# Four tiles in turn for the softmax statistics, and GpSimd and VectorE in ScalarE's place for the early normalisation

## The chip, the cores and the metric

The kernel runs on one core of a Trainium2 chip. The metric is the device time of one execution in microseconds (us), given as the median of several runs; lower is better. A profiled execution gives the trace, from which the rows further down are taken. The engines are named as the profile names them: PE is TensorE, ACT is ScalarE, DVE is VectorE, POOL is GpSimd, and SP is SyncE, which only issues transfers here. Each engine works through its own instructions strictly in order.

## The reference

Three stages follow one another: attention over a band of 64 keys, a gated feed-forward layer, and a second feed-forward layer with a leaky activation.

```python
# q, k, v: 4 batches, 8 heads, 576 positions, 64 wide
scores = (q @ k.T) / sqrt(64)                       # per batch and head
scores = where(0 <= pos_q - pos_k < 64, scores, -1e9)
attn = exp(scores - max(scores)); attn /= sum(attn) + 1e-9
x = (attn @ v)  -> 2304 tokens x 512
x = (silu(x @ w_gate) * (x @ w_val)) @ w_out        # 512 -> 1536 -> 512
h = x @ w2_in                                       # 512 -> 2048
out = maximum(0.01 * h, h) @ w2_out                 # 2048 -> 512
```

The weights arrive in 64-bit floats.

## The kernel before

**Attention in jobs.** The 2304 tokens are cut into five blocks of up to 512 columns. The attention of a block is done by eight jobs (one for a pair of heads and a part of the block). Jobs 0 to 7 make the first block and are the early ones: nothing else can begin before them. Their tokens are two halves of 256: jobs 0 to 3 make part 0, jobs 4 to 7 part 1. A job is a chain of steps over four tiles of 128 by 128:

- `natural` transposes q and k on PE and copies the result out of PSUM (on DVE for jobs 0, 1, 4, 5, on ACT for the others).
- `scores` (L210 to L229) multiplies on PE (L221), adds the mask and takes the row maxima on DVE (L226, called the reduction below), and on ACT takes the exponential with the row sums (L228). Maxima go to row 0 and sums to row 1 of a small tile `st`.
- `norm` (L231 to L243) adds 1e-9 to the sums (L235), takes the reciprocal (L236), both on DVE, and multiplies each of the four tiles by it: on ACT (L239), DVE (L241) or POOL (L243).
- `transpose` turns the tiles on PE (L249) and ACT copies them out (L253); `values` multiplies by v on PE (L266) and writes x (ACT L275, DVE L276).

**Buffers of a job.** The score tiles `e`, the transposed q and k and the transposed scores of an early job lie in one of four sets of rooms, in turn. The statistics tile `st` has one buffer for all jobs. In PSUM, jobs 0 to 3 have a bank each; all that jobs 4 to 7 put into PSUM, with the q and k transposes and the v products of every job, goes through one pair of buffers named `att`.

**The first feed-forward layer.** Its weights come in 36 tiles, three (gate, value, out) for each of the 12 slices f of the hidden width. A weight tile is fetched by SP into one of three raw buffers (L292), made into 32-bit floats by ACT (L302) and DVE (L304, L305), and split into a high and a low half by ACT (L312) and DVE (L313). A step (part, f) on PE is twelve matmuls for gate (pg), twelve for value (pv) and twelve for the output (acc), all on L560; between them ACT and DVE make the gated product (L604, L605, L612, L614), and POOL its low half (L615). In the first block the order of steps is (0,0), (0,1), (0,2), (0,3), (0,4), (1,0), (0,5), (1,1), (0,6), and so on to (1,11), so part 1 of x is first needed at the sixth step.

**What sets the order.** Each piece of work has a due time in slots (three slots to a step). A planner places each engine's instructions by these due times and its own reckoning of when each is ready. In `scores`, `norm`, `transpose` and `values` the work that is not PE's is moved ahead by 9.4 slots (`soon`), so that attention goes before weight tiles where both are ready.

**The later attention** (jobs 8 and up) shares one set of rooms for `e` in any case, and is normalised on ACT or, in some jobs, on POOL.

Of the kernel before, what the change touches and what calls it, by code (L numbers as in the profile page):

```python
# [8 lines left out]
F32 = mybir.dt.float32  # L9
# [4 lines left out]
P = 128  # L14
# [13 lines left out]
def banded_attention_moe_moe(  # L28
# [12 lines left out]
    nc = tc.nc  # L41
# [28 lines left out]
    ap = ctx.enter_context(tc.tile_pool(name="ap", bufs=1))  # L70
# [61 lines left out]
    def soon():  # L132
        prio(now[0] - 9.4)

    def load_nat(b, src, a, h0, h1, queue=nc.sync):
        for m in range(2):
            queue.dma_start(out=nat[:, a, m, h0:h1],
                              in_=src[b, h0:h1, m * P:(m + 1) * P, :].rearrange("h p d -> p h d"))

    def load_nv(b):  # L140

        for i in range(3):
            nc.sync.dma_start(out=nv[i], in_=v[b, :, 64 * i:64 * i + P, :].rearrange("h p d -> p h d"))

    def in_turn(mm):

        tc.keep_in_program_order(mm)

    class Job:
# [59 lines left out]

        def scores(self, i):  # L210
            if i == 0:
                self.st = ap.tile([P, 4, 6], F32, tag="st", name="st")
            st, e = self.st, self.e
            ps = (ps_acc if self.n < 4 else ps_att).tile([P, 4, P], F32, tag=self.bank, name="s")
            for a, t in enumerate(self.fills[i]):
                w0 = 64 * (t if self.half else max(t - 1, 0))
                if not self.early:
                    in_turn(nc.tensor.matmul(ps[:, a], lhsT=qbd[:, t, :], rhs=kT[:, w0:w0 + P], start=True, stop=True))  # L218
                    continue
                for r in (slice(0, 64), slice(64, 128)):  # L220
                    nc.tensor.matmul(ps[r, a], lhsT=self.kq[r, 256 + 64 * t:320 + 64 * t], rhs=self.kq[r, w0:w0 + P],  # L221
                                     start=True, stop=True)
            soon()
            for a, t in enumerate(self.fills[i]):
                mask = masks[:, 1 if (t == 0 and not self.half) else 0, :]
                nc.vector.tensor_tensor_reduce(out=e[:, t], in0=ps[:, a], in1=mask, scale=-0.125, scalar=3.0e38,  # L226
                                               op0=ALU.add, op1=ALU.min, accum_out=st[:, 0, t:t + 1])
                nc.scalar.activation(e[:, t], e[:, t], AF.Exp, bias=st[:, 0, t:t + 1], scale=-1.0,  # L228
                                     accum_out=st[:, 1, t:t + 1])  # L229

        def norm(self, i, engine):  # L231
            soon()
            ts, st, e = self.fills[i], self.st, self.e
            a, z = ts[0], ts[-1] + 1
            nc.vector.tensor_scalar(st[:, 2, a:z], st[:, 1, a:z], 1.0e-9, None, op0=ALU.add)  # L235
            nc.vector.reciprocal(st[:, 3, a:z], st[:, 2, a:z])  # L236
            for t in ts:
                if engine is nc.scalar:
                    nc.scalar.activation(e[:, t], e[:, t], AF.Copy, scale=st[:, 3, t:t + 1])  # L239
                elif engine is nc.vector:  # L240
                    nc.vector.tensor_scalar(e[:, t], e[:, t], st[:, 3, t:t + 1], None, op0=ALU.mult)  # L241
                else:
                    nc.gpsimd.tensor_scalar(e[:, t], e[:, t], st[:, 3, t:t + 1], 1.0, op0=ALU.mult, op1=ALU.mult)  # L243
# [245 lines left out]
    for blk, members in enumerate(BLOCKS):  # L489
        for n in range(2 * HP):  # L490
            i, hp = (n // HP, n % HP) if blk == 0 else (n % 2, n // 2)
# [6 lines left out]
    def at(slot, fn):  # L498
        plan.append((slot, len(plan), fn))
# [12 lines left out]
    for n, j in enumerate(jobs):  # L512
        nxt = jobs[n + 1] if n + 1 < len(jobs) else None
        if j.early:
            t = 2.4 * min(n, 4) + 3 * max(0, n - 4)
            E = lambda r, f, t=t: at(t + r - 17.3, f)
            E(0.0, j.natural)
            E(1.5, lambda j=j: j.scores(0))
            E(4.6, lambda j=j: j.norm(0, (nc.vector, nc.gpsimd, nc.scalar)[min(j.n, 2)]))
            E(6.3, lambda j=j: j.transpose(0))  # L520
            E(7.8, j.values)
            if n == 3:
                E(0.1, lambda: [load_nat(1, src, a, 0, H) for src, a in ((k, 0), (q, 1))])
                E(7.9, lambda: load_nv(1))
            if n == 7:
                E(7.9, nxt.load)
                E(7.9, lambda n=n: [jobs[n + a].load_v(True) for a in (1, 2)])
            continue
        i = n - min(jj.n for jj in jobs if jj.blk == j.blk)
        b0 = FIRST[j.blk - 1] + int(4.5 * i) + (29 if j.blk == 1 else -5)  # L530
        L = lambda r, f, b0=b0: at(b0 + r, f)
        L(0, j.quadrants)
        if nxt:
            L(0, nxt.load)

        s, m, t, w = (2, 4, 5.6, 8.7) if j.blk == 1 else (1.2, 3, 4.4, 7.2)
        for i in range(len(j.fills)):
            L(s + 0.4 * i, lambda j=j, i=i: j.scores(i))
            on = nc.scalar if j.blk > 1 or j.T < 5 else nc.gpsimd
            L(m + 0.2 * i, lambda j=j, on=on, i=i: j.norm(i, on))  # L540
            L(t + 0.2 * i, lambda j=j, i=i: j.transpose(i))
        if j.first:
            L(w, j.values)
            if nxt:
                L(w, lambda n=n: [jobs[n + a].load_v() for a in (1, 2)])
# [94 lines left out]
    for blk in range(1, NBLK):  # L640
        for f in range(NF1):
            slot = FIRST[blk] + 3 * f
            step1(slot, blk, slice(0, WIDTH[blk]), f, f == 0, f == NF1 - 1)
            i = NF1 * (blk - 1) + f
# [170 lines left out]
    for n, (i, fp) in enumerate(units):  # L815
# [19 lines left out]
        if n == 1:  # L835
            for j in (10, 11):
                space[j] = wp.tile([P, 3072], F32R, tag=f"w{j}", name=f"space{j}")
        t = {k: pool.tile([P, 448 if pool is tp else 512], F32, tag=tag, name=k)[:, 0:HALF]
             for k, pool, tag in (("t1", tp, "t"), ("u2", up, "u"), ("t5", tp, "g0"), ("u3", up, "u"), ("c", tp, "g1"))}
# [112 lines left out]
```

## Time and profile before

| | |
|---|---|
| median of 3 runs | 931.12 us (930.8 to 931.42) |
| profiled execution, its own time | 928.26 us |
| its span, first to last instruction | 926.3 us |
| PE busy in the span | 906.5 us (98%) |
| DVE, ACT, POOL busy | 662.3, 473.1, 350.5 us |
| mean granted clock of PE | 0.994 |

The span is the stretch that the trace covers, and all times in the rows are counted from its start. The profiled execution's own time lies 1.96 us over its span, and 2.86 us under the median.

### The profile page before, as it was taken

What the parts mean: (1) busy time and instruction counts of PE and PEld (TensorE: products, weight loads), DVE (VectorE), ACT (ScalarE), POOL (GpSimd) and SP (SyncE); (2) the same over time, 40 slices, a digit from 0 to 9 for tenths busy, and PEclk for the clock granted to TensorE, in tenths of its full rate; (3) what the DMA queues carried; (4) which work ended last, traced back from release to release, by engine and by line L of the source; (5) the groups of instructions that cost most, each with busy time, mean ns of one, the idle gap of its engine ahead of it and who ended that gap; (6) DMA issues with size and microseconds to landing.
All of it is one profiled execution on the core that took longest, in us unless ns stands there. A gap on an engine that the chain in (4) does not pass through costs nothing.

```text
span 926.3 us, 18141 instructions
## 1 busy us (share of the span) xinstructions
PE 906.5 (98%) x6147; PEld 858.6 (93%) x6147; DVE 662.3 (72%) x1529; ACT 473.1 (51%) x1181; POOL 350.5 (38%) x492
## 2 busy tenths in 40 slices
PE   7899899999999999999999999999999999999998
PEld 5788899999999999999999999999999999999997
DVE  5889854456666566656654464899998999978787
ACT  6976644545555555545543344635545445454342
POOL 1021322112122212222222123866668556675555
PEclk9899999999999999999999999999999999999999
DMA  9787433336566666656545694887559874588752
GB/s 245 209 221 232 130 56 59 90 85 187 185 195 169 206 193 176 195 163 179 168 162 190 250 319 134 265 252 243 160 178 294 263 249 128 165 268 265 246 159 80
DMA packets 198524, 176.32 MB, mean 190 GB/s; under 512 B 118048, under 2 KB 146976, under 8 KB 198432
## 3 DMA queue, kind: packets, MB, share of 16 engines
q1 hardware_dynamic: 196288, 174.64, 62.1%
q8 instruction: 49, 0.80, 0.4%
q10 hardware_dynamic: 2144, 0.52, 0.3%
q14 instruction: 43, 0.35, 0.1%
HBM read 135.27 MB, written 39.85 MB: 189 GB/s over the span
## 4 chain that ended last, share of the span: by engine, by line
PE 90%; DMA 4%; ACT 2%; DVE 2%; issue 1%; POOL 0%; ACTq 0%; SPq 0%; DVEq 0%; POOLq 0%
PE pg L560 15%; PE pv L560 15%; PE acc L560 15%; PE y L720 13%; PE px L677 8%; PE pw L677 5%; PE py L677 5%; PE yc L720 5%; DMA raw<-in_moe_w_val_dram 3%; PE s L218 3%; PE pv L266 2%; PE pt L249 2%; DMA raw<-in_moe_w_out_dram 1%; PE s L221 1%; DVE u L305 1%
## 5 line engine op out<-in xcount | busy, mean ns | idle before, releaser
L615 POOL TENSOR_TENSOR g<-th,g 128x448 fp32r<-128x448 f32 (+1 forms) x72 | 78.5, 1090 | 313.4 <-ACT g L614 284.6
L560 PE MATMUL pv<-x,w 128*128 128x448 f32 (+1 forms) x864 | 174.3, 345 | 4.9 <-DVE th L612 2.9
L560 PE MATMUL pg<-x,w 128*128 128x448 f32 (+1 forms) x864 | 172.4, 344 | 4.7 <-ACT x L275 3.0
L560 PE MATMUL acc<-g,w 128*128 128x448 f32 (+1 forms) x864 | 167.7, 340 | 1.6 <-POOL g L615 1.3
L560 PEld LDWEIGHTS pg<-x,w 128*128 128x128 f32 x864 | 144.1, 190 | 15.1 <-ACT x L275 3.4
L560 PEld LDWEIGHTS pv<-x,w 128*128 128x128 f32 x864 | 143.1, 190 | 15.7 <-DVE th L612 4.0
L560 PEld LDWEIGHTS acc<-g,w 128*128 128x128 f32 x864 | 144.5, 189 | 12.1 <-POOL g L615 2.5
L720 PE MATMUL y<-space,g 128*128 128x256 f32 x1035 | 145.6, 282 | 0.0
L720 PEld LDWEIGHTS y<-space,g 128*128 128x128 f32 x1035 | 137.9, 190 | 0.5 <-DVE space L714 0.3
L714 DVE TENSOR_TENSOR space<-y,space 128x512 f32<-128x512 f32 (+1 forms) x180 | 102.5, 593 | 11.5 <-PE y L720 10.7
L699 POOL TENSOR_TENSOR g<-t,g 128x384 fp32r<-128x384 f32 x71 | 77.9, 1099 | 56.5 <-ACT g L698 44.6
L677 PE MATMUL px<-space,space 128*128 128x384 f32 x432 | 89.1, 337 | 0.0
L605 DVE SCALAR_TENSOR_TENSOR th<-th,pg 128x448 f32<-128x448 f32 (+1 forms) x72 | 39.7, 551 | 62.1 <-ACT th L604 61.6
L677 PEld LDWEIGHTS px<-space,space 128*128 128x128 f32 x432 | 74.2, 188 | 1.0 <-DVE t L909 0.6
L614 ACT CAST g<-th 128x448 fp32r<-128x448 f32 (+1 forms) x72 | 37.0, 513 | 65.7 <-DVE th L612 65.7
L302 ACT ACTIVATE u<-raw 128x512 f32<-128x512 f32 x68 | 45.8, 676 | 47.8 <-DMA raw<-in_moe_w_out_dram 15.9
L699 POOL TENSOR_TENSOR g<-c,g 128x384 fp32r<-128x384 f32 x47 | 50.7, 1079 | 39.0 <-ACT g L698 26.9
L720 PE MATMUL yc<-space,g 128*128 128x256 f32 x414 | 63.7, 281 | 0.0
L677 PE MATMUL py<-space,space 128*128 128x384 f32 x288 | 63.5, 336 | 0.0
L677 PE MATMUL pw<-space,space 128*128 128x384 f32 x288 | 62.8, 336 | 0.0
L228 ACT ACTIVATE e<-e,st 128x128 f32<-128x128 f32 x120 | 46.9, 392 | 26.1 <-DVE st L226 26.1
L304 DVE TENSOR_SCALAR raw<-raw 128x512 int32<-128x512 int32 x68 | 29.4, 433 | 42.2 <-ACT u L302 34.1
(145 smaller groups left out, 1479.8 us busy)
## 6 DMA issues: line engine op xcount, KB each, us to landing
space<-o SPq DMA_DIRECT2D x147, 256.0 KB, 3.4
space<-a SPq DMA_DIRECT2D x140, 256.0 KB, 3.7
raw<-in_moe_w_out_dram SPq DMA_DIRECT2D x28, 512.0 KB, 4.9
a<-hl SPq DMA_DIRECT2D x24, 512.0 KB, 3.0
o<-hl SPq DMA_DIRECT2D x24, 512.0 KB, 3.1
raw<-in_moe_w_in_dram SPq DMA_DIRECT2D x16, 512.0 KB, 4.7
raw<-in_moe_w_gate_dram SPq DMA_DIRECT2D x12, 512.0 KB, 4.3
raw<-in_moe_w_val_dram SPq DMA_DIRECT2D x12, 512.0 KB, 4.7
```

The source lines that it names most:

```text
L218: in_turn(nc.tensor.matmul(ps[:, a], lhsT=qbd[:, t, :], rhs=kT[:, w0:w0 + P], start=True, stop=True))
L228: nc.scalar.activation(e[:, t], e[:, t], AF.Exp, bias=st[:, 0, t:t + 1], scale=-1.0, accum_out=st[:, 1, t:t + 1])
L302: nc.scalar.activation(u, f32(high), AF.Prelu, scale=EXP_SCALE, alpha=NEGATIVE)
L304: nc.vector.tensor_single_scalar(part, low, 29, op=ALU.logical_shift_right)
L560: nc.tensor.matmul(ps, lhsT=w(a, c), rhs=x(b, c), start=(start and n == 0), stop=(stop and n == 3 * len(cs) - 1), skip_group_check=True)
L605: nc.vector.scalar_tensor_tensor(out=th, in0=th, scalar=1.0, in1=pg, op0=ALU.add, op1=ALU.mult)
L614: nc.scalar.copy(g[0][:, :n], th)
L615: nc.gpsimd.tensor_tensor(g[1][:, :n], th, f32(g[0][:, :n]), op=ALU.subtract)
L677: nc.tensor.matmul(ps, lhsT=A2[n, k][:, a, c * P:c * P + P], rhs=X2[i, c, k][:, b], start=start and m == 0, stop=m == 5, skip_group_check= ...
L699: (lo or nc.gpsimd).tensor_tensor(g[:, 1], src, f32(g[:, 0]), op=ALU.subtract)
L714: nc.vector.tensor_tensor(f32(dst), ps, f32(dst), op=ALU.add)
L720: nc.tensor.matmul(ps, lhsT=g[:, a, r * P:r * P + P], rhs=O2[n, k][:, b], start=start and m == 0, stop=m == 2, skip_group_check=True)
```

## The change

The statistics tile gets four names in turn, by the job's number modulo 4, so that four jobs can each have one. The normalisation of a job takes a list of four engines, one for each tile, instead of one engine. Job 0 keeps DVE for its four tiles. Jobs 1 to 3 take POOL, DVE, POOL, DVE (job 1 had POOL for all four, jobs 2 and 3 had ACT). Jobs 4 to 7 take POOL for all four (they had ACT). The later jobs keep the engines that they had.

```diff
             if i == 0:
-                self.st = ap.tile([P, 4, 6], F32, tag="st", name="st")
+                self.st = ap.tile([P, 4, 6], F32, tag=f"st{self.n % 4}", name="st")
...
-        def norm(self, i, engine):
+        def norm(self, i, engines):
             soon()
...
-            for t in ts:
+            for t, engine in zip(ts, engines):
...
-            E(4.6, lambda j=j: j.norm(0, (nc.vector, nc.gpsimd, nc.scalar)[min(j.n, 2)]))
+            engines = [nc.vector] * 4 if n == 0 else [nc.gpsimd, nc.vector] * 2 if n < 4 else [nc.gpsimd] * 4
+            E(4.6, lambda j=j, engines=engines: j.norm(0, engines))
...
-            L(m + 0.2 * i, lambda j=j, on=on, i=i: j.norm(i, on))
+            L(m + 0.2 * i, lambda j=j, on=on, i=i: j.norm(i, [on] * 4))
```

## Rows read from the trace of the kernel before

**Rows 1.** The page: busy times, and busy tenths in 40 equal slices.

```profile
PE 906.5 (98%) x6147; PEld 858.6 (93%) x6147; DVE 662.3 (72%) x1529; ACT 473.1 (51%) x1181; POOL 350.5 (38%) x492
...
DVE  5889854456666566656654464899998999978787
ACT  6976644545555555545543344635545445454342
```

**Rows 2.** Stages: length, busy time of each engine, granted clock, DMA share, GB/s.

```profile
15.00:40.00 25.00, 18.28 (x151) 14.62 (x149) 20.79 (x71) 24.14 (x75) 0.99 (x2) 0.80 0.85 219
40.00:65.00 25.00, 23.12 (x210) 20.97 (x206) 22.50 (x62) 22.06 (x63) 5.49 (x8) 1.00 0.78 220
65.00:110.00 45.00, 40.73 (x317) 38.48 (x318) 39.98 (x89) 29.45 (x66) 10.54 (x14) 1.00 0.70 210
110.00:926.00 816.00, 812.24 (x5368) 774.49 (x5367) 572.51 (x1279) 389.62 (x960) 330.12 (x448) 1.00 0.61 187
```

**Rows 3.** PE's waits from 15 to 66.4 us: total, times, longest.

```profile
PE pg L560 <- ACT x L275: 3.0, 2, 2.6
PE pv L560 <- ACT w L312: 2.1, 1, 2.1
PE pv L560 <- DVE th L612: 1.2, 2, 0.6
```

**Rows 4.** PE's timeline: start, length, instruction (scores of jobs 3, 5, 7; steps).

```profile
12.70 0.43 PE L221 MATMUL s<-rooms 64*64 64x128 f32 x2
...
30.02 1.09 PE L221 MATMUL s<-nat 64*64 64x128 f32 x16
...
48.48 1.09 PE L221 MATMUL s<-rooms 64*64 64x128 f32 x16
...
61.46 1.70 PE L560 MATMUL pv<-x,w 128*128 128x256 f32 x12 [0.60 <-DVE th L612]
...
66.36 1.36 PE L560 MATMUL pg<-x,w 128*128 128x256 f32 x10
```

**Rows 5.** DVE's timeline: first reductions of jobs 3, 5, 7; one weight split.

```profile
21.28 0.29 DVE L226 CUSTOM_DVE_ANT_0 rooms<-s,masks 128x128 f32<-128x128 f32 x1 [0.49 <-ACT rooms L239]
...
34.33 0.29 DVE L226 CUSTOM_DVE_ANT_0 nat<-s,masks 128x128 f32<-128x128 f32 x1
...
50.72 0.29 DVE L226 CUSTOM_DVE_ANT_0 rooms<-s,masks 128x128 f32<-128x128 f32 x1
...
57.90 0.65 DVE L313 TENSOR_TENSOR w<-u,w 128x512 fp32r<-128x512 f32 x1
```

**Rows 6.** ACT's timeline: job 2's normalisation and what follows it.

```profile
19.97 1.28 ACT L239 ACTIVATE rooms<-rooms,st 128x128 f32<-128x128 f32 x4
21.15 0.60 ACT L312 CAST w<-u 128x512 fp32r<-128x512 f32 x1
```

**Rows 7.** One stage for L239 alone: length, ACT busy, clock, DMA share, GB/s.

```profile
15.00:60.00 45.00, 7.79 (x24) 0.89 0.81 218
```

**Rows 8.** Single lines: shortest, median, longest ns; first and last start.

```profile
L241 DVE TENSOR_SCALAR e<-e,st x4: 280/282/286, 9.7 to 10.3; 128x128 f32<-128x128 f32 x4
...
L243 POOL TENSOR_SCALAR nat<-nat,st x4: 369/377/802, 14.1 to 15.6; 128x128 f32<-128x128 f32 x4
...
L313 DVE TENSOR_TENSOR w<-u,w x36: 648/686/1240, 14.6 to 110.3; 128x512 fp32r<-128x512 f32 x36
```

**Rows 9.** POOL's timeline: job 1's normalisation, and a later low half.

```profile
14.13 1.86 POOL L243 TENSOR_SCALAR nat<-nat,st 128x128 f32<-128x128 f32 x4 [10.98 <-ACT pT L253]
...
107.20 1.02 POOL L615 TENSOR_TENSOR g<-th,g 128x256 fp32r<-128x256 f32 x1 [1.27 <-ACT g L614]
```

**Rows 10.** DVE's timeline beside these two stretches of POOL.

```profile
14.56 0.83 DVE L313 TENSOR_TENSOR w<-u,w 128x512 fp32r<-128x512 f32 x1 [0.62 <-ACT w L312]
...
106.00 0.43 DVE L304 TENSOR_SCALAR raw<-raw 128x512 int32<-128x512 int32 x1 [1.36 <-DMA raw<-in_moe_w_val_dram]
...
107.55 0.96 DVE L304 TENSOR_SCALAR raw<-raw 128x512 int32<-128x512 int32 x1
```

## The prediction

> **What bounds the kernel now.** I read the page first. PE is busy for 98% of the span, so over the whole run it is the bound, and the other engines matter only where they make PE wait. ACT's and DVE's slices are fullest at the left edge [rows 1], so I asked next for stages. From 110 us to the end PE is busy for 812.24 of 816 us at full clock [rows 2]: nothing that the change does there can shorten more than 3.8 us. What can be gained lies before 110. From 15 to 65 us PE is idle for 50 - 18.28 - 23.12 = 8.6 us, and from 65 to 110 for 4.3 us. In the first of these stages the granted clock is 0.80 on average: part of the stretch runs at the lower of the two levels, 1.2 GHz. At full clock its 18.28 busy us could be as little as 18.28 x 0.80 = 14.6, so the clock holds at most another 3.7 us. The ceiling of any gain before 65 us is thus 8.6 + 3.7 = 12.3 us.
>
> The waits of PE in that stage come next. The longest are for x, the output of the early attention (ACT L275, 3.0 us), and for a weight half that ACT had not made yet (2.1 us) [rows 3]. Both come from ACT, which is busy for 24.14 + 22.06 = 46.2 of the 50 us, and in 15 to 40 for 24.14 of 25 [rows 2]: ACT's queue sets the pace there. DVE is close behind, with 43.3 of 50.
>
> The timelines of PE and DVE show the second cause, which no list of waits names well. The score matmuls of job 3 end at 12.70 + 0.43 = 13.13 us, and its reduction on DVE begins at 21.28, 8.15 us later; the row says that it ended a wait for ACT's normalisation, which is job 2's [rows 4, 5]. That is the single `st`: the reduction writes what the earlier job's normalisation still reads. For job 5 the same distance is 34.33 - 31.11 = 3.2 us, for job 7 it is 50.72 - 49.57 = 1.15 us.
>
> **What leaves ACT.** Jobs 2 to 7 took 24 instructions of L239 off ACT's queue [rows 7]. Their 7.79 us of busy time overlap at the ends; four of them hold the queue from 19.97 to 21.15, so 1.18 us a job [rows 6], and six jobs 7.1 us. Since ACT is the pace in this stage, that is what ACT alone would give back.
>
> **What leaves the order.** With four `st` the reductions need no longer wait for the normalisation before. The 8.15, 3.2 and 1.15 us don't add to ACT's term, since during them ACT and DVE worked on weight tiles that are needed too; they let attention go first. For jobs 4 to 7 the pair of `att` buffers in PSUM still links a job to the one before (transposes, scores, transposed scores and v products all pass through it), so these jobs come closer but not free. The later jobs share `e` and gain nothing from `st`: 0, covered by the fact that PE waits for next to nothing after 110 us [rows 2].
>
> **What is added.** DVE gets two tiles in each of jobs 1 to 3. L241 starts every (10.3 - 9.7) / 3 = 0.2 us [rows 8], so six cost 1.2 us. POOL gets 6 + 16 = 22 tiles where it had 4. At the median of 0.377 us they are 8.3 us, and POOL is busy for only 6.5 of the 50 us from 15 to 65 [rows 2], so its time is free. Its latency isn't: four tiles take 1.86 us on POOL [rows 9] against 1.18 on ACT, 0.7 us more in each of jobs 4 to 7. I cost that at nothing, since ACT took its turn only when its queue let it, and the removed queue is worth more; were that cover gone it would be 4 x 0.7 = 2.8 us. Queued behind a normalisation on POOL are only the low halves L615, whose consumer, acc, comes a step later; ACT's copy L253 waits for the transposes, and behind it on ACT stand weight tiles.
>
> **What POOL does to DVE.** While POOL normalised job 1, one of its tiles took 0.802 instead of 0.377 us, and DVE's L313 beside it took 0.83 instead of its median 0.686 [rows 8, 9, 10]: 0.15 us lost to DVE for four tiles. That is the lower bound, 22 / 4 x 0.15 = 0.8 us. The upper comes from L304, which took 0.96 instead of 0.43 us beside a POOL instruction of 1.02 us [rows 9, 10]: DVE lost 0.53, 52% of POOL's time. On 22 x 0.377 = 8.3 us that is 4.3 us. I take 2 us, nearer to the row of the same instruction.
>
> The Trainium skill, in "SBUF — State Buffer", section "SBUF: two separate sides", says that VectorE and GpSimd share a pair of ports as an exclusive lock: an instruction of VectorE with two inputs in SBUF, or in a two-port mode, and one of GpSimd exclude one another for the whole instruction. The two stretched DVE rows agree with this; by it most of POOL's 8.3 us could fall on DVE, which is the first rival below.
>
> **The sum.** ACT would allow 7.1 us. DVE has 50 - 43.3 = 6.7 us idle from 15 to 65; less 1.2 and less 2.0 it has 3.5 us to be pressed together by, if it must do the same work in that time. It must not do quite all: the value tile of slice 4 was split by 57.90 + 0.65 = 58.55 us and used by PE at 61.46 [rows 4, 5], so weights run 2.9 us ahead of their use at the tightest step that I found, and DVE may lag by that much: 3.5 + 2.9 = 6.4 us. Between 3.5 and 6.4 I take 5.0 us, under ACT's 7.1 and far under PE's 12.3. It should show as step (1,0), which begins at 66.36 us [rows 4], beginning near 61. I leave the 4.3 us of idle PE from 65 to 110 as they are, and the rest of the run too. The profiled execution took 928.26 us, 1.96 over its span and 2.86 under the median; against its own span this makes 926.3 - 5.0 = 921.3 us, against the median 931.12 - 5.0 = 926.1 us. With both ends of the contention the DVE term moves from 1.2 + 0 to 4.7 + 2.9, a gain of 1.2 to 7.6 us, or 923.5 to 929.9 us.
>
> **Rivals.**
> - *POOL and DVE block each other, and the kernel gets slower.* The place is DVE from 15 to 65 us. DVE can take 6.7 - 1.2 = 5.5 us; that is used up when each of the 22 tiles costs it 5.5 / 22 = 0.25 us. If each costs its full 0.377 us, DVE overruns by 8.3 - 5.5 = 2.8 us, and weights and attention come that much later: 933.9 us. For it speaks that L304 and L313, the two that were stretched, each come with all 36 weight tiles, so that POOL will meet them often; against it, that job 1's four tiles cost 0.15 us in all.
> - *Hidden: the weights set the pace.* Attention goes ahead of weights by its due times. The reductions of jobs 5 to 7 that move forward are 3 x 4 x 0.29 = 3.5 us of DVE work [rows 5] put before weight tiles that have 2.9 us to spare; PE then waits for weights where it waited for x. The `att` pair pulls the same way, as it holds jobs 4 to 7 in line without `st`. The gain is 0 to 1.5 us: about 930.5 us.
> - *Larger.* x of part 0 is what PE waits for longest, and job 3 alone could come up to 8.15 us sooner. If PE then doesn't fall idle before 40 us, it keeps the higher clock as well, and gets most of 12.3 us: 10 us, or 921 us. Against it stands DVE's 6.4.
>
> **How the numbers follow.** A run of this kernel can tell about 0.2%, 1.9 us, from no change. The forecast (923.5 to 929 us) has 0.53, the larger gain 0.14, the hidden one 0.18, the slower one 0.15. Faster by over 0.2% is thus 0.67, within 0.2% 0.18, slower 0.15. For 8 in 10 the range takes in the forecast, the hidden case and some of both outer ones: 921 to 932 us.
>
> **What would show it.** In the profile after, L239 should be gone before 65 us and job 3's reduction begin within 2 us of 13 us. ACT's busy share from 15 to 55 should stay high with less to do, step (1,0) begin at 59 to 64, and L243 have 22 tiles there, mostly under 0.5 us. From 110 us on PE should be as full as now. I am wrong if DVE is busy without a gap and its L304, L305 and L313 are stretched (first rival), if PE's waits turn from x to w or u at an unchanged (1,0) (second), or if the planner's new order makes ACT or DVE stand waiting for a transfer in front of work that is ready.

## The result and the profile after

The changed kernel takes 936.13 us, median of 5 runs (934.4 to 938.02), against 930.99 us for the kernel before on the same chip: a ratio of 1.0065, with a 95% interval of 1.0053 to 1.0077. The medians lie 5.1 us apart, and by the ratio it is 6.0 us slower, where 5 us less was forecast.

The profiled execution after took 938.02 us, the longest of its five, with a span of 936.3 us; it lies 9.8 us over the profiled execution before, more than the medians do. First the busy times of the page:

```profile
PE 908.1 (97%) x6147; PEld 859.9 (92%) x6147; DVE 662.0 (71%) x1535; ACT 465.2 (50%) x1157; POOL 361.1 (39%) x510
...
DVE  6887844446766665656665463899998998978787
ACT  7675544545545545555543243644445436454442
```

ACT is busy for 7.9 us less than before [rows 1], as the 24 removed instructions promised [rows 7], and DVE for no more. So the work moved where it was meant to go, and the time went up all the same. The stages of after, with the columns of [rows 2]:

```profile
15.00:40.00 25.00, 16.21 (x117) 12.55 (x117) 20.08 (x61) 18.16 (x50) 5.38 (x8) 0.72 0.84 223
40.00:65.00 25.00, 19.37 (x174) 17.15 (x173) 21.41 (x59) 19.33 (x52) 7.72 (x12) 0.94 0.78 223
65.00:110.00 45.00, 39.49 (x318) 37.38 (x317) 35.45 (x72) 26.49 (x53) 10.12 (x17) 1.00 0.69 202
110.00:150.00 40.00, 38.34 (x353) 37.52 (x352) 21.15 (x89) 19.04 (x68) 11.11 (x23) 1.00 0.26 46
```

From 15 to 65 us PE is idle for 50 - 16.21 - 19.37 = 14.4 us, against 8.6 before [rows 2]: 5.8 us more. From 65 to 110 it is 5.5 against 4.3, and from 110 to 150 there are 1.7 us where before had none. The granted clock is lower as well: 0.72 against 0.80 up to 40 us, 0.94 against 1.00 up to 65. At the same time ACT is busy for only 37.5 of the 50 us, against 46.2, and DVE for 41.5 against 43.3. All three engines do less in this stage; nothing has become a new bound by being busy. Something stands and waits. PE's longest waits from 15 to 66.4 us (total, times, longest):

```profile
PE pg L561 <- ACT x L275: 3.7, 1, 3.7
PE pg L561 <- DVE th L606: 3.2, 2, 1.9
```

x was the longest wait before too [rows 3], and it has grown; that for the product with the tanh (L605 on ACT, then L606 on DVE; L604 and L605 before) is new. The first one, followed into PE's and ACT's timelines:

```profile
32.80 0.29 PE L266 MATMUL pv<-rooms,nat 128*64 128x64 f32 x4
36.75 0.58 PE L561 MATMUL pg<-x,w 128*128 128x256 f32 x1 [3.66 <-ACT x L275]
...
60.80 1.70 PE L561 MATMUL pg<-x,w 128*128 128x256 f32 x12 [1.92 <-DVE th L606]
...
73.03 1.60 PE L561 MATMUL pg<-x,w 128*128 128x256 f32 x12
```

```profile
32.47 0.70 ACT L302 ACTIVATE u<-raw 128x512 f32<-128x512 f32 x1 [1.07 <-DMA raw<-in_moe_w_val_dram]
33.06 0.61 ACT L312 CAST w<-u 128x512 fp32r<-128x512 f32 x1
35.25 0.67 ACT L302 ACTIVATE u<-raw 128x512 f32<-128x512 f32 x1 [1.58 <-DMA raw<-in_moe_w_out_dram]
35.82 0.60 ACT L312 CAST w<-u 128x512 fp32r<-128x512 f32 x1
36.33 0.37 ACT L275 CAST x<-pv 128x256 fp32r<-128x256 f32 x1
38.46 0.69 ACT L302 ACTIVATE u<-raw 128x512 f32<-128x512 f32 x1 [1.76 <-DMA raw<-in_moe_w_gate_dram]
39.03 0.41 ACT L228 ACTIVATE nat<-nat,st 128x128 f32<-128x128 f32 x1
```

This is the central reading, with lines of the trace after (PE above, ACT below). Job 3's v product is done on PE at 32.80 + 0.29 = 33.09 us. The copy of x, 0.37 us long, starts on ACT at 36.33, because the conversion of an out tile stands ahead of it in ACT's order, and ACT idles for 1.58 us until that tile's transfer lands. PE stands for 3.66 us. The same place in the trace before:

```profile
31.42 0.29 PE L266 MATMUL pv<-rooms,nat 128*64 128x64 f32 x4
34.35 0.39 PE L560 MATMUL pg<-x,w 128*128 128x256 f32 x1 [2.65 <-ACT x L275]
```

```profile
32.77 1.27 ACT L239 ACTIVATE e<-e,st 128x128 f32<-128x128 f32 x4
33.95 0.35 ACT L275 CAST x<-pv 128x256 fp32r<-128x256 f32 x1
```

There the v product is done at 31.71 us, and the copy comes behind a normalisation at 33.95. So x of job 3 comes 2.4 us later after the change: its v product is 1.4 us later, and ACT takes 1.0 us more to come to it. Further on in the trace after, the next conversion waits 1.76 us for a gate tile, with job 5's exponentials (L228) behind it. Step (1,0) begins at 73.03, 6.7 us later than before [rows 4] and 12 later than forecast. From 15 to 75 us ACT's waits for transfers are (total, times, longest; after, then before):

```profile
ACT u L302 <- DMA raw<-in_moe_w_out_dram: 3.9, 4, 1.6
ACT u L302 <- DMA raw<-in_moe_w_val_dram: 3.5, 4, 1.2
ACT u L302 <- DMA raw<-in_moe_w_gate_dram: 3.1, 4, 1.8
```

```profile
ACT u L302 <- DMA raw<-in_moe_w_val_dram: 3.0, 2, 2.0
ACT u L302 <- DMA raw<-in_moe_w_gate_dram: 1.7, 3, 0.6
ACT u L302 <- DMA raw<-in_moe_w_out_dram: 1.1, 2, 0.6
```

That is 10.5 us, where the kernel before has 3.0 + 1.7 + 1.1 = 5.8. On DVE the same happens on a smaller scale; in its timeline the product that PE waits for at 60.80 comes behind a weight tile:

```profile
13.82 0.28 DVE L226 CUSTOM_DVE_ANT_0 rooms<-s,masks 128x128 f32<-128x128 f32 x1
...
59.99 0.43 DVE L304 TENSOR_SCALAR raw<-raw 128x512 int32<-128x512 int32 x1 [0.21 <-DMA raw<-in_moe_w_out_dram]
...
60.33 0.41 DVE L606 SCALAR_TENSOR_TENSOR th<-th,pg 128x256 f32<-128x256 f32 x1
```

The first line of it is job 3's first reduction, at 13.82 against 21.28 us before [rows 5]: the four `st` freed it, as forecast. POOL's normalisations of jobs 4 to 7 are these:

```profile
32.87 3.06 POOL L243 TENSOR_SCALAR e<-e,st 128x128 f32<-128x128 f32 x4 [12.90 <-DVE st L236]
...
41.73 2.46 POOL L243 TENSOR_SCALAR nat<-nat,st 128x128 f32<-128x128 f32 x4 [5.80 <-ACT w L312]
...
48.35 2.88 POOL L243 TENSOR_SCALAR rooms<-rooms,st 128x128 f32<-128x128 f32 x4 [2.98 <-DVE st L236]
...
64.65 2.11 POOL L243 TENSOR_SCALAR rooms<-rooms,st 128x128 f32<-128x128 f32 x4 [8.26 <-ACT x L275]
```

2.11 to 3.06 us for four tiles, against 1.86 for job 1 before [rows 9] and 1.18 on ACT [rows 6]. Taken one by one, 11 of the 22 tiles took under 0.5 us, eight of them 0.37, and the other 11 took 0.53 to 1.42 us. Each of the longer ones ran beside L304, L305 or L313 on DVE. Two of the short ones ran beside L304 as well, and there it was L304 that took 0.50 and 0.52 us instead of 0.42. The longest, from 41.73 us, ran beside these two:

```profile
41.70 1.29 DVE L313 TENSOR_TENSOR w<-u,w 128x512 fp32r<-128x512 f32 x2
```

The eight L313 beside a POOL tile took 0.66 to 0.70 us, no more than the others: here it was mostly POOL that stood. That could be a cause of the loss as well, so it was tried.

What changed in ACT's order can be counted from the two traces: how many weight tiles ACT had begun to convert (L302) when it came to x of each job and to the tanh of each step. The third line is of an experiment further down.

```
conversions before    x of job 0..7               tanh of steps 1..5
kernel before         1  3  5  7 10 14 16 18       9 11 13 15 18
changed               1  3  6  9 12 17 18 21      10 13 17 18 21
early_edges           1  3  4  6  9 13 15 16       7  9 11 15 15
```

The planner put two more weight tiles ahead of x of job 3, three ahead of x of job 5, and four ahead of the third tanh. That it did so because ACT has time free is argued and not shown.

### The profile page after: what moved, and what is told of

The parts are those of the page before. It is cut to its first block, busy times and chain, and to the rows that moved or that the text cites. A ratio compares the mean times of both kernels' runs of the same rounds, so it can differ in the third digit from the quotient of the medians.

```text
span 936.3 us, 18128 instructions
## 1 busy us (share of the span) xinstructions
PE 908.1 (97%) x6147; PEld 859.9 (92%) x6147; DVE 662.0 (71%) x1535; ACT 465.2 (50%) x1157; POOL 361.1 (39%) x510
## 4 chain that ended last, share of the span: by engine, by line
PE 87%; DMA 6%; DVE 4%; ACT 1%; issue 1%; POOL 0%; SPq 0%; ACTq 0%; DVEq 0%; POOLq 0%
PE pv L561 15%; PE acc L561 15%; PE pg L561 14%; PE y L721 13%; PE px L678 8%; PE pw L678 5%; PE py L678 5%; PE yc L721 5%; DMA raw<-in_moe_w_val_dram 4%; PE s L218 2%; PE pv L266 2%; DMA raw<-in_moe_w_gate_dram 1%; PE pt L249 1%; DVE u L305 1%; DMA raw<-in_moe_w_out_dram 1%
## 5 line engine op out<-in xcount | busy, mean ns | idle before, releaser
L606 DVE SCALAR_TENSOR_TENSOR th<-th,pg 128x448 f32<-128x448 f32 (+1 forms) x72 | 39.7, 551 | 64.9 <-ACT th L605 64.6
L302 ACT ACTIVATE u<-raw 128x512 f32<-128x512 f32 x68 | 45.6, 675 | 57.1 <-DMA raw<-in_moe_w_in_dram 16.4
L304 DVE TENSOR_SCALAR raw<-raw 128x512 int32<-128x512 int32 x68 | 29.8, 439 | 46.1 <-ACT u L302 34.7
L228 ACT ACTIVATE e<-e,st 128x128 f32<-128x128 f32 x120 | 46.9, 392 | 27.4 <-DVE st L226 27.3
```

Of the source, the lines that this page charges most:

```text
L302: nc.scalar.activation(u, f32(high), AF.Prelu, scale=EXP_SCALE, alpha=NEGATIVE)
L304: nc.vector.tensor_single_scalar(part, low, 29, op=ALU.logical_shift_right)
L606: nc.vector.scalar_tensor_tensor(out=th, in0=th, scalar=1.0, in1=pg, op0=ALU.add, op1=ALU.mult)
```

## Experiments

Two theories. **Order:** the loss is the new order on ACT and DVE, in which conversions whose transfers have not landed stand ahead of attention and tanh. **POOL:** the loss is POOL's slow normalisation, or what POOL takes from DVE. "Edges" below are constraints on the planner that say which of two instructions on one engine is issued first; they add no wait between engines. The planner places all other instructions anew around them, PE's too. CONV[i] is the conversion of weight tile i (L302 on ACT, L304 on DVE), X[n] the copy of job n's x, EX[n] its last exponential, TH[s] the tanh and the product of step s, all counted from 0. Each edge stands for both engines unless it ends in [0], which is ACT alone. An edge names one weight tile, and says nothing of the tiles behind it.

### The parts of the change (e1_st, e2_engines)

Only the four `st`, and only the engines:

```diff
-                self.st = ap.tile([P, 4, 6], F32, tag="st", name="st")
+                self.st = ap.tile([P, 4, 6], F32, tag=f"st{self.n % 4}", name="st")
```

> The kernel before with the four statistics tiles alone; the engines of the normalisation stay as they were. Order theory (the planner reckons that weight tiles land sooner than they do; where ACT has free time in its reckoning it puts weight conversions, L302, ahead of x, exponentials and tanh, and on the chip these stand behind a wait for a transfer): in ACT's order the last x of part 0 comes after 7 conversions, as in the kernel before (9 in the changed one), and the second tanh after 12 (11 before, 13 changed), so 929 to 933 us. POOL theory (what POOL's normalisation costs through its latency, its lock with DVE and its queue makes the loss): no POOL tile is added and the reductions are freed, so a gain, 925 to 929 us.

```diff
-                self.st = ap.tile([P, 4, 6], F32, tag=f"st{self.n % 4}", name="st")
+                self.st = ap.tile([P, 4, 6], F32, tag="st", name="st")
```

(the second on the changed kernel)

> The changed kernel with one statistics tile for all jobs again; the new engines stay. Order theory: the last x of part 0 after 8 conversions and the second tanh after 11, between before and changed: 931 to 935 us. POOL theory: all POOL tiles are there and the freed reductions are not: 936 us or more.

Four `st` alone: 931.6 us, 1.0021 [1.0006, 1.0036]. The engines alone: 934.6 us, 1.0041 [1.0026, 1.0056]. Each part loses by itself, and 0.0021 + 0.0041 is near the whole 0.0065. The freed reduction is worth nothing alone, and the larger part of the loss comes with the engines. In e1 no work leaves ACT; x of job 3 keeps its place there, and the second and third tanh move behind 12 and 14 conversions.

### POOL's share (e3_act47, e4_dve47)

The changed kernel, with jobs 4 to 7 normalised on ACT as before, or on DVE (`[nc.vector] * 4` in the same place):

```diff
-            engines = [nc.vector] * 4 if n == 0 else [nc.gpsimd, nc.vector] * 2 if n < 4 else [nc.gpsimd] * 4
+            engines = [nc.vector] * 4 if n == 0 else [nc.gpsimd, nc.vector] * 2 if n < 4 else [nc.scalar] * 4
```

> The changed kernel, with jobs 4 to 7 normalised on ACT as before; only jobs 1 to 3 keep POOL and DVE. Order theory: the last x of part 0 still comes after 9 conversions and the second tanh after 14 (13 in the changed kernel): 934 to 938 us, as slow as changed. POOL theory: 16 of the 22 POOL tiles are gone, and the marks and low halves on POOL are no longer behind them: 931 us or less.

> The changed kernel, with jobs 4 to 7 normalised on DVE, 16 x 0.2 = 3.2 us more there. Order theory: the last x of part 0 still after 9 conversions and the second tanh after 13: 934 to 938 us. POOL theory: without lock and latency of these tiles 931 us or less, up to 3 us of it lost to DVE's added work.

934.69 us, 1.0043 [1.0024, 1.0062], and 935.86 us, 1.0057 [1.0042, 1.0072]. With POOL's sixteen tiles gone two thirds of the loss (e3) or nearly all of it (e4) is still there, where the POOL theory asked for 931 us or less. It falls as the main cause, also because l1_again below keeps all 22 POOL tiles and is faster than the kernel before. Whether the third that e3 gives back is real is not settled: its interval overlaps that of the change.

### The changed order on the kernel before (f2_before_late)

The helper with which every edge below is set, and the first set of them:

```python
def behind(later, earlier):                 # order of issue only, no wait
    tc.add_manual_dep(later, earlier.name, mybir.DependencyInfo(
        mybir.DependencyClass.NoSync, mybir.DependencyReason.DATA), reason="order")
```

The engines and `st` of before, and edges that put ACT and DVE into the changed kernel's order up to the third tanh:

```python
for later, earlier in ((X[2], CONV[5]), (X[3], CONV[8]), (TH[0], CONV[9]), (X[4], CONV[11]),
                       (TH[1], CONV[12]), (TH[2], CONV[16])):
    for engine in range(2):
        behind(later[engine], earlier[engine])
behind(EX[5], CONV[9][0]); behind(EX[6], CONV[10][0])
```

> The kernel before, one statistics tile and its old engines, with edges that give it the order of the changed kernel: last x of part 0 after 9 conversions, the first three tanh after 10, 13 and 17. Order theory: it gets the loss without the change: 934 to 938 us. POOL theory: no POOL tile is added, 929 to 932 us.

933.82 us, 1.0052 [1.0037, 1.0067]: a little under what the order theory asked for. Not an instruction differs from the kernel before, only the order, and 4.5 us are lost. The order differs on PE too: in the kernel before, six gate and value matmuls from 28.73 us on stand ahead of job 5's score matmuls at 30.02 [rows 4], here they stand behind them, and PE waits 1.42 us ahead of the scores:

```profile
30.05 1.09 PE L223 MATMUL s<-nat 64*64 64x128 f32 x16 [1.42 <-DVE nat L203]
31.07 0.38 PE L565 MATMUL pg<-x,w 128*128 128x256 f32 x1
```

Its stages:

```profile
15.00:40.00 25.00, 17.70 (x134) 14.15 (x132) 20.94 (x69) 23.79 (x72) 1.47 (x3) 0.73 0.89 227
40.00:65.00 25.00, 19.46 (x171) 17.35 (x168) 20.55 (x61) 20.83 (x60) 3.58 (x7) 0.93 0.73 213
```

PE is down to 17.70 and 19.46 us and the granted clock to 0.73 and 0.93, as in the changed kernel. Here ACT hardly stands waiting (23.79 of 25 us busy up to 40), and its waits for transfers from 15 to 75 us are 4.5 us, less than the 5.8 of the kernel before: work that PE needs later stands ahead of work that it needs now, whether the transfer has landed or not. So the waits for transfers can't be the whole of the loss; l1_again, further down, has 7.8 us of them and gains.

Nor does the loss need the lower clock, whatever that adds here. In e3 PE is busy for less time up to 40 us than in any of the three, at a higher clock than in the kernel before, and 4 us are lost all the same:

```profile
15.00:40.00 25.00, 14.89 (x121) 11.04 (x121) 20.78 (x64) 20.65 (x59) 2.32 (x4) 0.87 0.85 228
```

### The order of before on the changed kernel (f1_pinned)

```python
for later, earlier in ((CONV[5], X[2]), (CONV[7], X[3]), (CONV[9], TH[0]), (CONV[10], X[4]),
                       (CONV[11], TH[1]), (CONV[13], TH[2])):
    ...
behind(CONV[9][0], EX[5]); behind(CONV[11][0], EX[6])
```

> The changed kernel, with edges that only set the order of issue on ACT and DVE: the x, tanh and exponential instructions of the first 75 us again stand after as many weight conversions as in the kernel before (last x of part 0 after 7, the first three tanh after 9, 11 and 13). Order theory: the loss is in this order, so it goes: 926 to 931 us. POOL theory: POOL's tiles, lock and queue are as in the changed kernel, so 934 us or more.

933.62 us, 1.0055 [1.004, 1.007]: a miss. ACT's counts are those of before up to the third tanh, and most of the loss stays. So ACT's counts alone don't explain it. On DVE's timeline the third product still comes late:

```profile
53.61 0.43 DVE L308 TENSOR_SCALAR raw<-raw 128x512 int32<-128x512 int32 x1 [2.43 <-DMA raw<-in_moe_w_out_dram]
55.29 0.43 DVE L308 TENSOR_SCALAR raw<-raw 128x512 int32<-128x512 int32 x1 [1.25 <-DMA raw<-in_moe_w_gate_dram]
...
56.12 0.39 DVE L611 SCALAR_TENSOR_TENSOR th<-th,pg 128x256 f32<-128x256 f32 x1
```

(L308 and L611 are L304 and L606; the edges shift the lines.) The tanh itself ran on ACT at 52.40 us; the product comes 3.4 us after its end, in DVE's order behind two tiles that DVE waits for (2.43 and 1.25 us), and PE stands for 3.1 us. The tiles go gate, value, out, three to a slice, so the out tile is CONV[14] and the gate tile CONV[15]. The edge (CONV[13], TH[2]) holds, as CONV[13] comes on DVE at 56.43 us, but the planner moved the two tiles after it past it and ahead of the product. So the third product comes behind 15 tiles on DVE, where the kernel before has 14 (at 51.56 us): f1 restored ACT's order and not DVE's, and its miss speaks neither for nor against the order theory.

### Attention and every early tanh first (f3_pinned2, h1_before_pinned2)

```python
for later, earlier in ((CONV[4], X[2]), (CONV[6], X[3]), (CONV[7], TH[0]), (CONV[9], X[4]),
        (CONV[9], TH[1]), (CONV[11], TH[2]), (CONV[12], X[5]), (CONV[13], TH[3]),
        (CONV[14], X[6]), (CONV[15], TH[4]), (CONV[16], X[7])):
    ...
behind(CONV[7][0], EX[5]); behind(CONV[9][0], EX[6]); behind(CONV[12][0], EX[7])
```

On the changed kernel (f3), and the same edges on the kernel before (h1):

> The changed kernel, with edges that put attention and tanh one to two conversions earlier than in the kernel before (last x of part 0 after 6, the first three tanh after 7, 9 and 11). Order theory: faster than the run with the old order, and the gain that was forecast for the change comes out: 923 to 929 us. POOL theory: 934 us or more.

> The kernel before, with the same edges as the run that pins attention and tanh earliest. It tells what the order alone is worth, and by its distance to that run what the change is worth under one order. Order theory: 925 to 930 us, and 2 to 5 us above the changed kernel under the same edges, ACT's 7.1 us and the waits on the one statistics tile being the difference. POOL theory: 925 to 930 us too, but below the changed kernel under the same edges.

929.49 us, 1.0005 [0.9995, 1.0015], and 930.23 us, 1.0016 [1.0005, 1.0026]. On the changed kernel the whole loss is gone by order alone. The gain hoped for didn't come: the sixth tanh runs at 66.9 us (70.0 before, 79.2 in the changed kernel), but by the twelfth the lead is 1.4 us (99.15 against 100.57). Between the two kernels there are 0.7 us under these edges.

### Less work on DVE (j1_pinned_dve, j4_before_pinned_dve, j2_before_dve)

Does DVE hold the stage from 65 to 110 us? The low halves of the out tiles (L313) go to POOL, twelve of 36, which by the estimate in the expectations takes 12 x 0.6 = 7.2 us off DVE:

```diff
-    def split(hi, lo, u):
+    def split(hi, lo, u, eng=nc.vector):
         nc.scalar.copy(hi, u)
-        nc.vector.tensor_tensor(lo, u, f32(hi), op=ALU.subtract)
+        eng.tensor_tensor(lo, u, f32(hi), op=ALU.subtract)
...
-        split(w[:, 0], w[:, 1], u)
+        split(w[:, 0], w[:, 1], u, nc.gpsimd if c == "o" else nc.vector)
```

On f3, on h1, and on the kernel before without edges:

> The changed kernel with the edges that put attention earliest, and with the low half of each out tile (12 of the 36 instructions of L313) on POOL in place of DVE. It asks why the same kernel without that is no faster than the kernel before, though its sixth step comes 3 us sooner. If DVE paces the weight stream from 65 to 110 us, 12 x 0.6 = 7.2 us less on DVE keep the lead: 924 to 928 us. If the transfers through three raw buffers pace it: 928 to 931 us. POOL theory: 12 more long instructions on POOL, slower, 932 us or more.

> The kernel before with the same edges and the same 12 low halves on POOL. Its distance to the run of the changed kernel with both is what the change is worth where the order is held and DVE has room. Order theory: 0 to 5 us slower than that run. If the change had nothing to give at all: within 1 us of it.

> The kernel before with these 12 low halves on POOL and no edges. It takes 7.2 us of work off DVE, as the change took 7.1 off ACT, and the planner answers alike: last x of part 0 after 9 conversions, first tanh after 10, third after 15 (before 7, 9, 13). Order theory: freed time is again filled with weight tiles ahead of x, and the gain is lost: 930 to 936 us. If work taken off a full engine simply came back as time: 924 to 927 us.

928.89 us, 1.0 [0.9988, 1.0012]; 934.0 us, 1.006 [1.0044, 1.0076]; 932.67 us, 1.0042 [1.0028, 1.0057]. The relief is far smaller than the estimate. Over the run DVE's busy time fell by only 2.6 us (662.3 to 659.7 from the kernel before to j2, and 664.3 to 661.7 from f3 to j1), while POOL's rose by 14 to 17. From 65 to 110 us it did not fall at all, f3 first, j1 below:

```profile
65.00:110.00 45.00, 40.99 (x320) 38.58 (x319) 39.83 (x88) 28.95 (x66) 11.07 (x14) 1.00 0.73 216
```

```profile
65.00:110.00 45.00, 38.89 (x294) 36.70 (x295) 39.89 (x87) 29.29 (x66) 19.27 (x19) 0.96 0.72 220
```

So j1 leaves open whether DVE's time paces that stage. The third run looks like the changed kernel with other work: it is 4 us slower than the kernel before, and its planner moved x of job 3 behind the ninth conversion and the first tanhs behind 10, 13 and 15. What POOL's added work has in that loss is not separated. j4 is 5.1 us slower than j1 and does worse than h1, though its counts on ACT are those of h1; why is not known.

### Only the early edges (l1_pinned3, l1_again, m1_before_pinned3)

The first six pairs of f3 and the edges for EX[5] and EX[6], on the changed kernel (l1, twice) and on the kernel before (m1):

```python
for later, earlier in ((CONV[4], X[2]), (CONV[6], X[3]), (CONV[7], TH[0]), (CONV[9], X[4]),
                       (CONV[9], TH[1]), (CONV[11], TH[2])):
    ...
behind(CONV[7][0], EX[5]); behind(CONV[9][0], EX[6])
```

> The changed kernel with the early edges only: those up to the x of job 4 and the third tanh, from the run that pinned attention earliest; the order of what follows is left to the planner. Order theory: the loss grows from 25 to 65 us in the trace of the changed kernel, so most of it goes: 929 to 933 us; what is left over 929.5 is the loss of the later order. POOL theory: 934 us or more.

> The changed kernel with the early edges again, the same kernel as before, in 5 rounds. Order theory: 926 to 929 us, 0.1 to 0.3% under the kernel before. If the first measurement was chance: within 0.1% of the kernel before.

> The kernel before with the same early edges. What the change is worth under one order is its distance to the run above. If the four statistics tiles and ACT's 7.1 us are worth something once the order is held: 929 to 932 us, 2 to 4 us slower than the run above. If all of the gain above is the edges' own: within 1 us of it.

On the changed kernel 927.6 us, 0.9984 [0.997, 0.9999], and again 926.6 us, 0.9974 [0.9962, 0.9987]: faster than both kernels, and 1.3 and 2.6 us faster than the kernel before on the same chip. On the kernel before the same edges give 933.63 us, 1.0045 [1.003, 1.0061]. Beside l1_again, which ran on the same chip, that is 7.0 us. It is not a fixed worth of the change, since 4.4 us of it are what the edges cost the kernel before, and the same distance was 0.7 us from h1 to f3 and 5.1 us from j4 to j1. The stages of the two, l1_again first, m1 below:

```profile
15.00:40.00 25.00, 19.52 (x169) 15.58 (x165) 21.39 (x71) 21.75 (x64) 6.90 (x13) 0.86 0.85 223
40.00:65.00 25.00, 22.69 (x198) 21.03 (x198) 19.75 (x50) 15.85 (x39) 8.06 (x15) 0.93 0.69 200
65.00:110.00 45.00, 41.38 (x321) 38.63 (x320) 39.88 (x92) 30.05 (x69) 12.15 (x14) 1.00 0.72 216
```

```profile
15.00:40.00 25.00, 18.22 (x160) 14.44 (x160) 20.06 (x71) 24.62 (x78) 1.20 (x3) 0.86 0.79 214
40.00:65.00 25.00, 21.94 (x187) 20.61 (x186) 20.01 (x58) 19.60 (x54) 4.95 (x8) 0.93 0.70 199
65.00:110.00 45.00, 38.48 (x300) 36.58 (x299) 39.25 (x90) 29.09 (x64) 9.83 (x11) 0.96 0.74 221
```

In m1 ACT is full up to 40 us (24.62 of 25) and the edges only shift its load; in l1 it has 3.2 us free there, and PE is busier by 1.3, 0.8 and 2.9 us in the three stages. The edges pay on the changed kernel, where ACT has room; that the room is the reason is argued.

### POOL under the early edges, and one edge more (m2_pinned3_act, m3_pinned4)

l1 with jobs 4 to 7 on ACT (m2), and l1 with (CONV[13], TH[3]) added (m3):

> The changed kernel with the early edges and jobs 4 to 7 normalised on ACT. Under the held order POOL's theory gets its best case: if latency and lock on POOL take back part of the gain, this is 2 us or more faster than the run with the early edges alone. If taking 4.7 us off ACT is worth more than POOL costs, it is 0 to 3 us slower.

> The changed kernel with the early edges and one more, the fourth tanh ahead of the fourteenth conversion. In the run with the early edges this tanh came 11 us after the third. Order theory: 0 to 2 us faster than that run, 925 to 928 us; if transfers and DVE pace what follows, the same as it.

929.58 us, 1.0003 [0.9991, 1.0015], and 931.08 us, 1.0018 [1.0004, 1.0031]. POOL's four jobs are thus worth 929.58 - 926.6 = 3.0 us under these edges, which hold only a part of the order: the rest may differ between the two. The last is a miss: 4.5 us over l1_again from a single edge. In m3's profile ACT reaches the fourth tanh two conversions sooner than in l1, yet at the same 55 us; PE has a wait of 3.0 us for a product on DVE up to 103.85 us, and the granted clock up to 40 us is 0.80 against 0.86. On DVE, as in f1, a later tile (CONV[14]) slipped past the edge and ahead of the fourth product. Which of these makes up the 4.5 us is not settled.

## Why the prediction was wrong

- **Where the time is decided.** Right: it was won and lost before 110 us. The eleventh tanh runs at 93.96 us before, at 104.89 after (10.9 us later, in an execution that took 9.8 us longer), at 98.81 in f2 (4.9 later, 5.5 us longer) and at 92.85 in l1_again (1.1 earlier, 0.7 us shorter).
- **What leaves ACT.** Right: 24 instructions, 7.9 us of busy time. That the 7.1 us that ACT "would allow" stand close to the 7.0 us between m1 and l1_again is chance: that difference holds `st` and DVE's tiles too, and the same difference is 0.7 and 5.1 us under other edges.
- **What leaves the order.** Half right. Job 3's reduction began at 13.82 us, as forecast, but x of job 3 came at 36.33, later than before (33.95 in its trace). The text said that the stall lets attention go first; it freed DVE's step, and then ACT let weight tiles go first. Alone the four `st` cost 2 us.
- **POOL's latency at nothing.** Four tiles took 2.11 to 3.06 us, where 1.86 was reckoned with, and 11 of the 22 tiles were under 0.5 us, where "mostly" was forecast. The cost of nothing is not confirmed and was not what failed: l1_again carries it and is faster than the kernel before, and with these jobs on ACT it loses 3.0 us (m2).
- **What POOL does to DVE.** DVE is busy for 41.5 us from 15 to 65, not more than before, and with POOL's jobs moved to DVE itself (e4) the loss stayed. The term charged DVE with 2 us; in the trace after, the stretch fell mostly on POOL, and L313 beside it kept its 0.66 to 0.70 us. The first rival had the right sign and about half of the loss, by the wrong mechanism. The Trainium skill, "SBUF — State Buffer", section "SBUF: two separate sides", says that an instruction of VectorE with two inputs in SBUF, or in a two-port mode, and one of GpSimd exclude one another, and that the one that starts first goes ahead. The trace agrees in that each POOL tile over 0.5 us ran beside L304, L305 or L313. It doesn't agree throughout on who goes ahead: at 65.00 us a POOL tile began 0.05 us before an L313 and took 0.90 us, while that L313 took 0.69. No run here separates the rule from other causes of the stretch, and it isn't where the time went.
- **The sum: the step that failed.** "ACT would allow 7.1 us ... Between 3.5 and 6.4 I take 5.0 us" takes the order on ACT and DVE as fixed and presses it together. The planner placed the instructions anew, with more conversions ahead of x, exponentials and tanh; f2 shows that this order costs 4.5 us without any change to the work, and f3 that another order takes the whole loss away from the changed kernel. The last sentence of the prediction named this case, "the planner's new order makes ACT or DVE stand waiting for a transfer in front of work that is ready", but it had no price and no chance, so the range ended at 932 and missed.

**What stays open.** Shown: order alone costs the kernel before 4.5 us (f2) and takes the whole loss off the changed one (f3, l1); POOL isn't the main part of the loss; with the early edges the changed kernel is 1.3 to 2.6 us faster than the kernel before. Not shown: how much of f1's loss is DVE's order; which engine's order costs how much, since PE's moves with the others; why the lead of f3 fades from 65 to 110 us and why m3's edge costs. Whether the transfers through the three raw buffers set the pace there was not tried, as with a fourth buffer. Nor was a smaller path tried alone: in the changed kernel POOL's marks for job 8's loads (L285) come at 67.53 us behind job 7's normalisation, SP issues a gate fetch after them at 70.15, and ACT waits 4.35 us for that tile up to 76.72. e3 and e4 lose 4 and 5.3 us without it (their longest such waits from 60 to 80 us are 2.0 and 3.0 us), so the loss doesn't need it, but it may add to it.

## What to carry to other kernels

Where a scheduler orders the queues, time taken off a full engine is not time gained: ask which instruction moves up into it, whether its data have landed, and what PE needs that now stands behind it. Judge such a change with the order held as well as under the scheduler's own: here the changed kernel was 5 to 6 us slower without edges, and 0.7 to 7.0 us faster than the kernel before where both had the same edges. If the loss is order, a few edges that keep the attention and the tanh ahead of weight tiles can take it away; one more cost 4.5 us again. Read in the trace what slips past the edges: in f1 two later tiles did.

## What was not expected of the hardware

- The order of issue, with the same instructions, is worth 4.5 us of 929 (f2, m1), in f2 through several waits of PE of 1 to 2 us. The granted clock from 15 to 40 us doesn't sort the runs: 0.80 in the kernel before, 0.73 in f2, but 0.86 in m1 and 0.87 in e3, which lose as well.
- Twelve instructions fewer on DVE, 0.686 us each at the median [rows 8], took only 2.6 us off its busy time once POOL did them, at 1.3 to 1.6 us each (j2), and the kernel before became 0.42% slower.
- The same POOL instruction on 128 by 128 elements took 0.37 us or up to 1.42 us in the trace after, and each one over 0.5 us ran beside L304, L305 or L313 on DVE.
